# A new order for the first maxima of attention, fewer dummy matmuls among them, and other places for the first loads of W1

## The chip, the cores and the metric

The kernel runs on one core of a Trainium2 chip. The metric is the time of one execution in microseconds on the device; lower is better. Three runs of the kernel before gave 1216.57, 1216.64 and 1218.34 us, median 1216.64. One execution was profiled.

Short names of the engines and queues: PE is TensorE, PEld its weight loads, DVE VectorE, ACT ScalarE, POOL GpSimd, SP SyncE, which here issues most transfers (SPq is its queue).

## The reference

Attention over 8 x 8 heads with pooled queries, then a mixture of eight experts whose tokens are assigned by falling gate score under a cap.

```python
q_pool = q.reshape(B, H, S // 2, 2, D).mean(axis=3)          # B, H, S, D = 8, 8, 1152, 64
scores = q_pool @ k.T / sqrt(D)
scores = scores - max(scores, axis=-1)
attn = exp(scores); attn = attn / (sum(attn) + 1e-09)
x = (attn @ v) as [4608, 512]
logits = x @ w_gate                                          # 8 experts, 576 tokens each at most
for token, expert in order of falling logits: assign if both are free
out[tokens of e] = relu(x[tokens of e] @ w1[e]) @ w2[e]
```

## The kernel before

Attention treats two heads at a time, 32 pairs in all; then the experts run one after the other. Of a pair the work is: loads of keys (KD), queries (QD for the first pair, QS for the others) and values (VD); bounds, sums of absolute values or squares on ACT that give scales (`bounds`); a split of each number into two float16 parts (KH, KL, QH, QL; `split`, `values`); copies of these by SP's transfers into the forms that the score matmuls read (KA, KB, QA, QB, BD; `spread`); the maxima of the scores, one matmul into a PSUM bank and one reduction on DVE for each piece (`max_chunk`), folded by `max_end`, transposed on PE and written into a row of QB by `aug`, where they serve as bounds; then 18 steps (`step`), each with the scores of 128 keys on PE (L793), the exponential on ACT (L796), the low part PM on POOL or DVE (L800) and the weighted sum of values on PE (L810).

The first pair is treated in another way than the rest: its maxima are made head by head, 15 pieces of 384 columns for each head (5 blocks of queries, 3 thirds of the keys; `max_chunk` at n = 0), with a contraction over 64 rows. For the first head the banks rotate over ma, av0, sc0, av1 and sc1, by the number of the piece; for the second head over ma and mb. The written bound needs the constant ndiag, made on DVE by `fill` (L510) from a counter that POOL writes (L508). The later pairs need BD, a block-diagonal copy of QH, for their maxima (L710, L713).

Dummy matmuls of 512 columns (L948) stand in PE's order at the start: ten with the tag "wu" on av1, and as many as AT["wx"] says, 13, with the tag "wx" on av0. Their results are overwritten.

W1 is read once during attention, in 32 loads of 512 KB into the one buffer WB, each with a square on ACT that sums it (`weights`, L472 and L474, one for each pair). A load has to wait until the square of the load before has read WB.

The order of all this work on each engine is set by the class `Cycle`: an operation is given a number from the tables TAU0 (first pair), TAU1, TAU2 and TAU, by its tag and its count, and of the operations whose inputs are written in the order so far the one with the lowest number comes next. The engines and SP's queue each work through their part of that order in turn; an instruction that waits holds all behind it on its engine. In the tables "mm0" and "mr0" are the matmuls and reductions of the first head, "fill" the constants, "ldw" and "wsq" the load and the square of W1, "wx" the dummies, "scv" the scale of the values.

Of the kernel before, what the change touches and what calls it, by code (L numbers as in the profile page):

```python
# [159 lines left out]
class Cycle(Order):  # L160
# [11 lines left out]
    def plan(self):  # L172
# [58 lines left out]
        -31.28967, -16.54009, 11.37296, -165.2382, 7.395536, -8.984111, -4.211814], "expb": [-29.09149,  # L231
        -22.94875, -1.956318, -58.58073, -17.31112, 8.70511, -44.15053, -10.60943, -83.61574], "fill":
# [15 lines left out]
        [-32.42996, -52.99154], "sc": [-118.7466], "scv": [13.52603], "spr": [-12.95725, -60.11802, -17.91313,
        -33.7785, -32.93921, -13.53914, 7.216188, -42.886, 4.220658, -38.88641, -146.5483, -24.13281], "vd":
        [-49.85137, -34.44854], "vh": [8.519713, -90.95726], "vl": [-18.40057, -17.39675], "vs": [-142.1097,  # L250
        -10.46893, -117.9683, -53.38023], "vsh": [-33.54066], "wsq": [12.26831], "wu": [-17.875, -17.555,
        -17.235, -16.915, -16.595, -16.275, -15.955, -15.635, -15.315, -14.995], "wx": [-4.689, -4.369, -3.886,
        -3.403, -3.083, -2.763, -2.28, -1.797, -1.314, -0.994, -0.674, -0.354, -0.034], "x": [26.86098,
        -21.42417]}
TAU1 = {"abs": [-12.63603, -9.007276, -10.61048], "aug": [-9.325879], "augd": [-24.68238, -15.56411], "augt":
# [5 lines left out]
        "expa": [-31.62902, -34.53196, 7.506785, -5.098975, -3.698539, -9.956472, 18.47283, -146.9597,  # L261
        -8.541267], "expb": [-92.73379, -23.81719, -29.00838, -7.55417, 15.52308, 17.65719, 20.07963, -36.40239,
        -8.822007], "fold": [-67.48551], "kd": [-17.85042, -20.86023, -101.4387], "kh": [-21.38899, -13.56883],
        "kl": [-24.3647, -69.39262], "ld": [-38.975, -38.325], "ldq": [-40.925], "ldv": [-39.625], "ldw":
# [8 lines left out]
        7.957536, -30.97699, 26.53293], "qkb": [-134.6881, -19.11279, 4.672508, 7.631733, -18.85315, -7.293164,  # L273
        -146.6946, -45.59129, 22.34192], "ql": [-46.37856], "rc": [-86.19829, -10.06201], "sc": [-61.60109],
        "scv": [-12.29273], "spr": [-7.110299, -82.23665, -9.971891, -10.88851, -4.162817, -38.01306, -24.27872,
        -157.8473, -11.66528, -19.92012, 9.739897, -18.36458], "vd": [-13.48229, -158.5643], "vh": [-13.8261,
        -115.4854], "vl": [-32.5142, -145.3052], "vs": [-102.0759, -147.1307], "vsh": [-42.73812], "wsq":
# [1500 lines left out]
```

## Time and profile before

| | |
|---|---|
| median of three runs | 1216.64 us |
| the profiled execution | 1218.28 us |
| its span, first to last instruction | 1216.5 us |
| PE busy | 1183.1 us, 97% |
| DVE busy | 1000.1 us, 82% |
| ACT busy | 968.8 us, 80% |
| POOL busy | 903.2 us, 74% |

The profile gives the busy time of each engine and, in other views, each instruction with its start. Busy times of PE are modelled at their ends, since matmuls overlap: two matmuls in a row overlap in the rows by some 0.2 us. What stands in brackets behind a row of the order of time is the idle time of the engine before it and what ended that.

### The profile page before, as it was taken

How to read it: one execution, taken by the hardware profiler on the slowest of the kernel's cores; microseconds unless marked ns; L12 is line 12 of the kernel's file. 1: busy time of each engine (PE TensorE's matmuls, PEld its weight loads, DVE VectorE, ACT ScalarE, POOL GpSimd, SP SyncE). 2: the span in 40 equal slices, each digit the busy share in tenths (PEclk: the TensorE clock that was granted, in tenths of full speed). 3: DMA queues.
4: the chain of work that ended last, by engine and by line, in shares of the span. 5: the costliest groups of instructions: out<-in, count | busy, mean ns of one | idle time of the engine just before them, and what ended most of it. 6: DMA issues, size and time to landing. Idle time of an engine off the chain costs nothing.

```text
span 1216.5 us, 39132 instructions
## 1 busy us (share of the span) xinstructions
PE 1183.1 (97%) x15608; PEld 859.7 (71%) x15608; DVE 1000.1 (82%) x2689; ACT 968.8 (80%) x1712; POOL 903.2 (74%) x881
## 2 busy tenths in 40 slices
PE   7889999999999999999999999999999999999998
PEld 2667787787777787877777877776657566575673
DVE  6889999999999999999999996688888898883420
ACT  7868999999999999989988987246887677785851
POOL 6978898898889889888888888244685484676631
PEclk9999999999999999999999999999999999999999
DMA  8666777767777767667668642041453463546301
GB/s 254 155 148 175 174 180 189 175 174 192 174 177 192 168 176 199 166 174 202 163 167 204 162 106 70 22 178 53 165 198 129 147 206 129 165 138 239 118 31 39
DMA packets 131219, 190.84 MB, mean 157 GB/s; under 512 B 50268, under 2 KB 86108, under 8 KB 128732
## 3 DMA queue, kind: packets, MB, share of 16 engines
q1 hardware_dynamic: 117948, 126.75, 39.6%
q0 software_dynamic: 12944, 61.58, 17.3%
q8 instruction: 122, 2.00, 0.7%
q14 instruction: 61, 0.50, 0.1%
q10 hardware_dynamic: 144, 0.02, 0.0%
HBM read 116.41 MB, written 18.87 MB: 111 GB/s over the span
## 4 chain that ended last, share of the span: by engine, by line
PE 82%; DVE 11%; DMA 2%; issue 2%; ACT 1%; SPq 0%; POOL 0%; POOLq 0%; ACTq 0%; DVEq 0%
PE sc L793 21%; PE av L810 19%; PE ph L1661 12%; PE po L1693 11%; PE mb L710 5%; PE ma L710 5%; DVE MX L713 2%; DMA BD<-QH 1%; PE av L857 1%; PE po L1699 1%; PE av L871 1%; PE rt L1264 1%; PE rt L1224 1%; ACT P L796 1%; PE po L1706 1%
## 5 line engine op out<-in xcount | busy, mean ns | idle before, releaser
L800 POOL TENSOR_TENSOR PM<-P 128x576 f16<-128x576 f32 x508 | 611.7, 1265 | 99.1 <-ACT P L796 52.6
L796 ACT ACTIVATE P<-sc,EX 128x576 f32<-128x576 f32 x576 | 412.5, 739 | 77.7 <-PE sc L793 58.1
L810 PEld LDWEIGHTS <-P 128*128 128x128 bf16 x5760 | 293.0, 98 | 30.0 <-issue 1.9
L810 PE MATMUL av<-V,P 128*128 128x65 f16 (+1 forms) x5760 | 301.1, 192 | 0.0
L810 PE MATMUL av<-V,PM 128*128 128x65 f16 x2880 | 292.8, 194 | 0.0
L810 PEld LDWEIGHTS <-PM 128*128 128x128 f16 x2880 | 263.8, 97 | 0.0
L793 PE MATMUL sc<-QB,KB 65*128 65x288 f16 (+1 forms) x1152 | 235.7, 285 | 0.9 <-DMA QB<-AU 0.9
L793 PE MATMUL sc<-QA,KA 128*128 128x288 f16 x1152 | 234.5, 285 | 1.4 <-ACT P L796 1.3
L713 DVE TENSOR_REDUCE MX<-mb 128x1 f32<-128x512 f32 x279 | 190.7, 683 | 27.6 <-PE mb L710 22.6
L713 DVE TENSOR_REDUCE MX<-ma 128x1 f32<-128x512 f32 x279 | 190.6, 683 | 10.7 <-PE ma L710 7.9
L793 PEld LDWEIGHTS <-KA 128*128 128x128 f16 x1152 | 106.1, 97 | 74.2 <-issue 23.6
L1693 PE MATMUL po<-W2H,HX 128*128 128x512 f16 x512 | 155.7, 379 | 0.0
L1661 PE MATMUL ph<-XH,W1H 128*128 128x320 f16 (+1 forms) x512 | 145.5, 286 | 1.2 <-DVE XL L1518 0.9
L1661 PE MATMUL ph<-XH,W1L 128*128 128x320 f16 (+1 forms) x512 | 145.6, 286 | 0.0
L1661 PE MATMUL ph<-XL,W1H 128*128 128x320 f16 (+1 forms) x512 | 145.6, 286 | 0.0
L793 PEld LDWEIGHTS <-KB 65*128 65x128 f16 (+1 forms) x1152 | 112.5, 98 | 30.4 <-issue 1.1
L1693 PEld LDWEIGHTS <-HX 128*128 128x128 f16 x768 | 71.4, 98 | 79.2 <-issue 0.6
L1661 PEld LDWEIGHTS <-W1H 128*128 128x128 f16 x1024 | 97.5, 98 | 28.7 <-issue 5.3
L1715 POOL DMA_INDIRECT out_dram<-OT,idx x40 | 38.9, 971 | 104.8 <-ACT OT L1695 84.4
L710 PE MATMUL ma<-KH,BD 128*128 128x512 f16 x279 | 105.7, 379 | 4.7 <-DMA BD<-QH 2.0
L710 PE MATMUL mb<-KH,BD 128*128 128x512 f16 x279 | 105.5, 378 | 3.2 <-DVE MX L713 1.4
L1613 POOL TENSOR_TENSOR W2L<-W,W2H 128x512 f16<-128x512 f32 x64 | 73.0, 1159 | 35.2 <-ACT W L1611 31.9
(341 smaller groups left out, 2129.9 us busy)
## 6 DMA issues: line engine op xcount, KB each, us to landing
KD<-in_kt_dram SPq DMA_DIRECT2D x64, 288.0 KB
VD<-in_v_dram SPq DMA_DIRECT2D x32, 576.0 KB
WB<-in_w_dram SPq DMA_DIRECT2D x32, 512.0 KB
QA<-QH SPq DMA_DIRECT2D x128, 72.0 KB
KB<-KH SPq DMA_DIRECT2D x64, 144.0 KB
KA<-KH SPq DMA_DIRECT2D x64, 144.0 KB
KA<-KL SPq DMA_DIRECT2D x64, 144.0 KB
x_dram<-X SPq DMA_DIRECT2D x16, 576.0 KB
```

The source lines that it names most:

```text
L710: od.add(t, "PE", 214, lambda: nc.tensor.matmul(m, BD[i][:, j, :], KH[i][:, 512 * c:512 * c + 512], start=True, stop=True), r=bd + [("KH", ...
L713: od.add(t, "DVE", 597, lambda: nc.vector.tensor_reduce(MX[i][:, j, c:c + 1], m, axis=AX.X, op=OP.max), r=[mk], w=[("MX", i, j, c)], tag=" ...
L793: nc.tensor.matmul(c[:, t, :288], a[i][:rows, s, ks], b[i][:rows, s, 288 * t:288 * t + 288], start=first, stop=not first)
L796: od.add(g + 0.1, "ACT", 624, lambda: nc.scalar.activation(p.rearrange("p (t q) -> p t q", t=2), c[:, :, :288], AF.Exp, scale=EX[n % 3][:, ...
L800: od.add(g + 0.2, en, dur, lock=1, fn=lambda: eng.tensor_tensor(pm, p, hi, op=OP.subtract), r=[("P32", g % NP)], w=[("PM", g % NM)], tag="pm")
L810: nc.tensor.matmul(out, w[:, qs], v, start=kb == 0 and j == 0 and y == 0, stop=kb == NKB - 1 and y == 2, skip_group_check=True)
L857: nc.tensor.transpose(m[:, 128 * z:128 * z + 128], X[u][:, 3 * q + z], ident)
L871: nc.tensor.matmul(av[1][32 * q:32 * q + E, :384], wgs[:, c], XT[q].rearrange("p c t -> p (c t)"), start=True, stop=True)
L1613: od.add(tt, "POOL", 1230, lambda o=lo[p], a=raw[p], h=hi[p]: nc.gpsimd.tensor_tensor(o, a, h, op=OP.subtract), r=[key, hk, sk], w=[(nm + ...
L1661: nc.tensor.matmul(p, a[:, d, fs], b[:, d, qs], start=z == 0, stop=z == 11)
L1693: nc.tensor.matmul(o, a[:, z, q0:q0 + 128], b[:, z], start=z == 0 and y == 0, stop=z == 7 and y == 2)
L1715: st = nc.gpsimd.indirect_dma_start(out=out, out_offset=bass.IndirectOffsetOnAxis(ap=idx[i][:n, c:c + 1], axis=0), in_=OT[ob][:n], in_offs ...
```

## The change

Four things, nearly all of them by numbers in the tables:

- The 15 matmuls of the first head get numbers of their own, and the reductions numbers that let each come as soon as its matmul is in the order. The five pieces of the first third of the keys come first, over the five banks in turn, then three of the second third, then the two small matmuls of the values' bound, then the rest.
- AT["wx"] goes from 13 to 5. One of the five stands ahead of the last matmul of the head, four behind it.
- ndiag comes before the first reduction (it now also waits for the limit that `bounds` writes last, EL), and POOL's counter for it comes before the split's work.
- The loads of W1 for the first three pairs, and the square of the first, go elsewhere ("ldw" in three tables, "wsq" in TAU0). The values' scale of the first pair ("scv") has a new number too; on ACT the scale, the first pair's values and the second pair's bounds move up over the square that is gone there.

The diff, cut to its core (the tables are wrapped anew, most of its lines are that):

```diff
-        27.86655, 5.699136, -84.03057], "fold": [-87.75963, -168.3226], "kd": [-5.692977, -1.827225, -13.79063],
-        "kh": [-23.36129, -5.94297], "kl": [-2.127716, -36.39443], "ld": [-17.875, -16.575, -17.225], "ldv":
-        [-15.275], "ldw": [-12.675], "mm0": [-16.51403, -17.39233, -25.94788, -28.2417, -24.44536, -159.4969,
...
+        -16.575, -17.225], "ldv": [-15.275], "ldw": [12.2], "mm0": [-20, -19.95, -4.406, -19.99, -19.94,
+        -4.407, -19.98, -19.93, -4.41, -19.97, -4.412, -4.409, -19.96, -4.411, -4.408], "mm1": [-157.2919,
...
-      15, 16, 17], "d1": 2.0, "cw1": 0.7, "wx": 13, "wy": 0}
+      15, 16, 17], "d1": 2.0, "cw1": 0.7, "wx": 5, "wy": 0}
...
-            od.add(t + .4, "DVE", 370, lambda: nc.vector.tensor_scalar(ndiag, iq, 0.0, -1.0 / UP, op0=OP.is_equal, op1=OP.mult),
-                   r=["iq"], w=["ndiag"], tag="fill")
+            od.add(-55, "DVE", 370, lambda: nc.vector.tensor_scalar(ndiag, iq, 0.0, -1.0 / UP, op0=OP.is_equal, op1=OP.mult),
+                   r=["iq", ("EL", 0)], w=["ndiag"], tag="fill")
```

Lines of the changed kernel lie one lower than those of the kernel before from `routing_tables` on (L704 is L705 there). What the change makes of the order, at three places:

DVE, from the limit of the first pair on; MX is where the reductions write, av_169 is av1, av_168 av0, sc_166 and sc_167 are sc0 and sc1. Before:

```order
L595 TENSOR_SCALAR CB<-EX_116 128x1
L704 TENSOR_REDUCE MX_137<-av_169 128x1
L704 TENSOR_REDUCE MX_137<-sc_166 128x1
L704 TENSOR_REDUCE MX_137<-sc_167 64x1
L704 TENSOR_REDUCE MX_137<-av_168 128x1
L704 TENSOR_REDUCE MX_137<-ma 128x1
L704 TENSOR_REDUCE MX_137<-av_168 128x1
L704 TENSOR_REDUCE MX_137<-av_169 128x1
```

The same place in the changed kernel:

```order
L596 TENSOR_SCALAR CB<-EX_116 128x1
L511 TENSOR_SCALAR ndiag<-scratch 128x640
L705 TENSOR_REDUCE MX_137<-ma 128x1
L705 TENSOR_REDUCE MX_137<-av_168 128x1
L705 TENSOR_REDUCE MX_137<-sc_166 128x1
L705 TENSOR_REDUCE MX_137<-av_169 128x1
L705 TENSOR_REDUCE MX_137<-sc_167 64x1
L705 TENSOR_REDUCE MX_137<-ma 128x1
L571 TENSOR_SCALAR VE_135<-mb 128x1
L576 TENSOR_SCALAR VE_135<-VE_135 128x1
L705 TENSOR_REDUCE MX_137<-av_168 128x1
```

ndiag stands ahead of the reductions, and these go over the five banks in turn.

PE, the last matmuls of the first head; QH and KH are the operands, "ones" and "wide" those of the dummies. Before (behind the last row four more dummies and the transposition follow):

```order
L948 MATMUL av_168<-wide,ones 128x512
L701 LDWEIGHTS QH_89
L701 MATMUL ma<-KH_85,QH_89 128x384
L701 LDWEIGHTS QH_89
L701 MATMUL sc_166<-KH_85,QH_89 128x384
L948 LDWEIGHTS ones
L948 MATMUL av_168<-wide,ones 128x512
```

The same place in the changed kernel (behind the last row three more dummies and the transposition follow):

```order
L702 MATMUL sc_167<-KH_85,QH_89 64x384
L702 LDWEIGHTS QH_89
L702 MATMUL av_168<-KH_85,QH_89 128x384
L949 LDWEIGHTS ones
L949 MATMUL av_168<-wide,ones 128x512
L702 LDWEIGHTS QH_89
L702 MATMUL ma<-KH_85,QH_89 128x384
L949 LDWEIGHTS ones
L949 MATMUL av_168<-wide,ones 128x512
```

One dummy on av0 stands between the last two matmuls, where five stood ahead of both.

SP, the transfers around the fourth pair's BD (BD_102; QS_124 are queries of the fifth pair, the others copies for the third). Before:

```order
L659 DMA QA_98<-QH_90 64x576
L527 DMA QS_124<-in_qt_dram 128x576
L659 DMA QB_99<-QL_91 64x576
L472 DMA WB<-in_w_dram 128x1024
L659 DMA KB_95<-KH_85 64x1152
L659 DMA QB_99<-QL_91 64x576
L638 DMA BD_102<-QH_90 64x9x64 x2
```

The same place in the changed kernel:

```order
L660 DMA QA_98<-QH_90 64x576
L473 DMA WB<-in_w_dram 128x1024
L528 DMA QS_124<-in_qt_dram 128x576
L660 DMA QB_99<-QL_91 64x576
L660 DMA KB_95<-KH_85 64x1152
L660 DMA QB_99<-QL_91 64x576
L639 DMA BD_102<-QH_90 64x9x64 x2
```

Before, the load in this piece is the third of W1; in the changed kernel it is the second, and the third stands later, ahead of KB_96.

## Rows read from the trace of the kernel before

**Rows 1.** The page: busy us, share of the span, instructions of each engine.

```profile
PE 1183.1 (97%) x15608; PEld 859.7 (71%) x15608; DVE 1000.1 (82%) x2689; ACT 968.8 (80%) x1712; POOL 903.2 (74%) x881
```

**Rows 2.** Stretches: length, busy of PE, PEld, DVE, ACT, POOL, PEclk, DMA share, GB/s.

```profile
10.30:13.90 3.60, 3.56 (x10) 0.99 (x10) 2.50 (x5) 3.60 (x7) 3.31 (x4) 1.00 0.98 316
16.20:19.60 3.40, 3.40 (x11) 0.81 (x9) 2.40 (x7) 2.74 (x5) 2.67 (x8) 1.00 1.05 236
...
23.00:32.40 9.40, 8.68 (x53) 4.10 (x52) 7.16 (x17) 7.85 (x14) 7.68 (x7) 1.00 0.53 156
62.00:64.40 2.40, 1.34 (x8) 0.58 (x6) 1.93 (x4) 1.01 (x2) 1.94 (x2) 1.00 0.00 0
...
67.60:68.60 1.00, 1.00 (x25) 0.85 (x22) 0.83 (x5) 0.97 (x4) 0.38 (x1) 1.00 0.08 14
...
72.00:76.00 4.00, 4.00 (x96) 3.47 (x93) 3.95 (x8) 2.79 (x5) 3.55 (x4) 1.00 1.15 205
...
120.00:820.00 700.00, 693.24 (x11512) 552.08 (x11510) 629.32 (x1336) 602.27 (x1039) 583.73 (x524) 1.00 0.65 164
```

**Rows 3.** PE in order of time: start, length, operation, count, [idle before].

```profile
8.09 2.30 PE L948 MATMUL av<-wide,ones 128*128 128x512 bf16 x5
10.32 0.50 PE L701 MATMUL av<-KH,QH 64*128 64x384 f16 x1
...
17.61 2.12 PE L948 MATMUL av<-wide,ones 128*128 128x512 bf16 x5
...
20.09 1.25 PE L948 MATMUL av<-wide,ones 128*128 128x512 bf16 x5
21.61 0.30 PE L755 MATMUL mb<-ident,CM 128*69 128x128 f32 x1 [0.28 <-DVE CM L742]
...
23.20 0.42 PE L793 MATMUL sc<-QA,KA 128*128 128x288 f16 x2
```

**Rows 4.** DVE in order of time, first head's reductions and ndiag.

```profile
10.85 0.56 DVE L704 TENSOR_REDUCE MX<-av 128x1 f32<-128x384 f32 x1 [1.32 <-PE av L701]
...
16.43 0.14 DVE L570 TENSOR_SCALAR VE<-mb 128x1 int32<-128x1 int32 x1
...
17.71 0.55 DVE L704 TENSOR_REDUCE MX<-sc 64x1 f32<-64x384 f32 x1 [0.95 <-PE sc L701]
...
19.11 0.48 DVE L510 TENSOR_SCALAR ndiag<-scratch 128x640 f32<-128x640 int32 x1
20.19 0.56 DVE L704 TENSOR_REDUCE MX<-sc 128x1 f32<-128x384 f32 x1 [0.60 <-PE sc L701]
20.66 0.55 DVE L704 TENSOR_REDUCE MX<-ma 128x1 f32<-128x384 f32 x1
```

**Rows 5.** ACT in order of time, 61 to 70 us.

```profile
61.64 1.37 ACT L796 ACTIVATE P<-sc,EX 128x576 f32<-128x576 f32 x2 [1.67 <-POOL PM L800]
64.44 0.74 ACT L796 ACTIVATE P<-sc,EX 128x576 f32<-128x576 f32 x1 [1.43 <-PE sc L793]
...
66.36 1.06 ACT L474 ACTIVATE VJ<-WB 128x1024 bf16<-128x1024 f32 x1
...
69.27 0.76 ACT L625 ACTIVATE QH<-QS,SC 128x576 f16<-128x576 f32 x1
```

**Rows 6.** SP's queue in order of time: issues of transfers.

```profile
67.59 0.34 SPq L527 DMA_DIRECT2D QS<-in_qt_dram  x1
...
68.62 0.53 SPq L472 DMA_DIRECT2D WB<-in_w_dram  x1
...
70.41 1.38 SPq L638 DMA_DIRECT2D BD<-QH  x2
...
84.78 0.59 SPq L659 DMA_DIRECT2D KB<-KH  x1
```

**Rows 7.** The wait for BD: PE in order of time, then the chain.

```profile
78.93 0.38 PE L710 MATMUL ma<-KH,BD 128*128 128x512 f16 x1 [1.68 <-DMA BD<-QH]
...
71.07 7.73 DMA BD<-QH
```

More of the change, by code (lines that the diff above doesn't have):

```diff
@@ L226 @@
         [-124.0397, -148.4135], "av0a": [11.70915, -1.304429, -29.50539, 21.40864, 9.122039, 19.93749,
[4 rows of a table removed]
-        -31.28967, -16.54009, 11.37296, -165.2382, 7.395536, -8.984111, -4.211814], "expb": [-29.09149,
-        -22.94875, -1.956318, -58.58073, -17.31112, 8.70511, -44.15053, -10.60943, -83.61574], "fill":
[13 rows of a table removed]
-        -0.7874408, -89.24226, -30.95353, -90.94815, 19.75168], "qkb": [-38.71843, -25.8134, -10.06655, 9.20107,
-        -67.31496, -58.03232, -88.79007, 19.41297, 27.0304], "ql": [-118.7245], "qs": [-143.2866], "rc":
@@ L248 @@
[L248 to L252, printed above, removed]
@@ L253 @@
-        -3.403, -3.083, -2.763, -2.28, -1.797, -1.314, -0.994, -0.674, -0.354, -0.034], "x": [26.86098,
-        -21.42417]}
-TAU1 = {"abs": [-12.63603, -9.007276, -10.61048], "aug": [-9.325879], "augd": [-24.68238, -15.56411], "augt":
[5 rows of a table removed]
[L261 to L264, printed above, removed]
[8 rows of a table removed]
[L273 to L277, printed above, removed]
-        [11.82567], "x": [13.33649, -21.05682]}
[5 rows of a table added]
@@ new lines @@
+        "expb": [-29.09149, -22.94875, -1.956318, -58.58073, -17.31112, 8.70511, -44.15053, -10.60943,
+        -83.61574], "fill": [-101.4709, -108.6709, -122.5445, -31.35041, -28.09493, -30, -119, 1.012261,
+        -94.58812, 27.86655, 5.699136, -84.03057], "fold": [-87.75963, -168.3226], "kd": [-5.692977,
+        -1.827225, -13.79063], "kh": [-23.36129, -5.94297], "kl": [-2.127716, -36.39443], "ld": [-17.875,
+        -16.575, -17.225], "ldv": [-15.275], "ldw": [12.2], "mm0": [-20, -19.95, -4.406, -19.99, -19.94,
[8 rows of a table added]
@@ new lines @@
+        -33.38241, -13.43728, -8.625754, -0.787441, -89.24226, -30.95353, -90.94815, 19.75168], "qkb":
[4 rows of a table added]
+        [-18.40057, -17.39675], "vs": [-142.1097, -10.46893, -117.9683, -53.38023], "vsh": [-33.54066], "wsq":
+        [33], "wu": [-17.875, -17.555, -17.235, -16.915, -16.595, -16.275, -15.955, -15.635, -15.315,
+        -14.995], "wx": [-4.689, -4.369, -3.886, -3.403, -3.083, -2.763, -2.28, -1.797, -1.314, -0.994,
+        -0.674, -0.354, -0.034], "x": [26.86098, -21.42417]}
+TAU1 = {"abs": [-12.63603, -9.007276, -10.61048], "aug": [-9.325879], "augd": [-24.68238, -15.56411], "augt":
[6 rows of a table added]
+        -146.9597, -8.541267], "expb": [-92.73379, -23.81719, -29.00838, -7.55417, 15.52308, 17.65719,
[6 rows of a table added]
+        -17.17329, -28.31773, -186.4031, -92.20261, -88.02035, -139.6368, -4.943824, -77.30257], "mre":
[3 rows of a table added]
+        -2.967549, 5.094675, -84.92769, 8.738667, 10.78074, 7.957536, -30.97699, 26.53293], "qkb": [-134.6881,
[6 rows of a table added]
@@ L279 @@
 TAU2 = {"abs": [-28.66554, -33.20308, -33.07647], "aug": [-155.8978], "augd": [-31.13019, -15.26595], "augt":
         [-14.59994], "av0a": [5.912519, -33.47845, -26.79091, -27.48911, -29.13166, -8.697946, -24.82091,
[4 rows of a table removed]
-        [-36.73381, -17.79995, 11.0648, 12.05918, 4.224331, -49.88403, -79.15411, -73.20015, -78.03694], "expb":
-        [5.303638, -28.09439, -86.66189, 11.14589, 13.52404, 0.9933214, -108.1325, 17.65723, -12.04455], "fold":
-        [-76.7964], "kh": [-25.48746, -30.72508], "kl": [-85.91257, -137.1086], "ld": [-43.77507, -60.36052],
@@ L288 @@
-        "ldq": [-155.8887], "ldv": [-44.13215], "ldw": [-36.80441], "me": [-14.41274, -10.50764, -4.941736],
[7 rows of a table removed]
-        [3.525368, 5.485969, 7.082238, -29.81771, 16.89603, 17.62602, 19.72256, 21.49451, 25.15933], "qkb":
[4 rows of a table removed]
-        -140.0679], "vsh": [-156.7671], "wsq": [25.35071], "x": [-88.3642, 9.707762]}
[4 rows of a table added]
+        [-34.60962], "expa": [-36.73381, -17.79995, 11.0648, 12.05918, 4.224331, -49.88403, -79.15411,
+        -73.20015, -78.03694], "expb": [5.303638, -28.09439, -86.66189, 11.14589, 13.52404, 0.993321,
@@ new lines @@
+        -108.1325, 17.65723, -12.04455], "fold": [-76.7964], "kh": [-25.48746, -30.72508], "kl": [-85.91257,
+        -137.1086], "ld": [-43.77507, -60.36052], "ldq": [-155.8887], "ldv": [-44.13215], "ldw": [2.8], "me":
[8 rows of a table added]
+        19.72256, 21.49451, 25.15933], "qkb": [4.228648, -8.449217, 6.503895, 8.362543, 2.06596, 19.41358,
+        21.0541, 27.28868, 28.96957], "ql": [-13.86136], "rc": [-14.19222, -72.26224], "sc": [-157.8417],
+        "scv": [-26.20257], "spr": [-19.00547, -5.537296, -11.12926, -16.76412, -6.043836, -10.26983,
@@ L302 @@
+        -53.42223, -16.37789, -0.047992, -17.85246, -27.80794, -15.06558], "vh": [-108.6609, -34.0504], "vl":
+        [2.133735, -132.8829], "vs": [-32.43098, -140.0679], "vsh": [-156.7671], "wsq": [25.35071], "x":
+        [-88.3642, 9.707762]}
 AT = {"load": -11.1, "vload": -12.4, "split": -11.0, "bound": -10.3, "bq": 0.1, "bv": -0.1, "bs": 0.1, "spread": 4.1,
```

91 rows, old and new, of tables (TAU0, TAU1, TAU2) are left out of this document.

## The prediction

> **What bounds the kernel now.** I read the page's shares first: TensorE (PE) is busy 97% of the span, VectorE (DVE) 82% [rows 1]. Then the table of stretches: from 120 to 820 us PE is busy 693.24 of 700.00 us, but in 62 to 64.4 us only 1.34 of 2.40 [rows 2]. PE works in program order and is full later, so a microsecond is won or lost only where it still waits, in the first 100 us; what its queue gains there reaches the end. Everything the change moves lies there. So I read that stretch engine by engine, in order of time: PE [rows 3], DVE [rows 4], ScalarE (ACT) [rows 5], the SP queue [rows 6], and at last the one wait on a transfer that PE shows [rows 7].
>
> Two places count. **Place one** is the first head's maxima: 15 reductions on DVE from 10.85 us to the last start at 20.66 [rows 4], then PE's transposition at 21.61, then the first scores at 23.20 [rows 3]. **Place two** is PE's wait of 1.68 us for BD of the fourth pair, ended at 78.93; that transfer took 7.73 us [rows 7].
>
> **The clock at place one.** The granted clock reads 1.00 in every stretch, but the rows of one shape do not agree: five matmuls of 512 columns are 2.30 us long at 8.09, 2.12 at 17.61, and 1.25 at 20.09 [rows 3]. That is about 0.43 us each, 512 columns at 1.2 GHz, and then 0.21, at 2.4. So the clock rose shortly before 20 us. Before it PE was busy 3.40 of 3.40 us, with seven dummies in it, while 3.56 of 3.60 us of mostly 64-row maxima at 10.3 did not raise it [rows 2].
>
> **Part 1, the order over five banks.** Before, the maxima wait for matmuls that stand behind dummies and in shared banks: DVE is idle 1.32 us before the first, 0.95 before the one at 17.71, 0.60 before the one at 20.19, and the constant ndiag (0.48) stands among them at 19.11 [rows 4]. The first start stays at 10.85, since the five dummies ahead of it stay. A reduction takes the engine 0.47 us (20.19 to 20.66). After, fourteen reductions follow without a hole, as each matmul's bank was read three or more places earlier, and the two small steps of the values' bound cost some 0.15 each (0.14 at 16.43 [rows 4]): the fourteenth starts at 10.85 + 13 x 0.47 + 0.31 = 17.27 and ends 0.55 later, at 17.82. The fifteenth is not free: one dummy on the same bank stands between the fourteenth's matmul and its own on PE, so it waits for reduction 14, the dummy, its matmul and two hand-overs of some 0.05. At 2.4 GHz (0.21 + 0.18) it starts at about 18.35, at 1.2 GHz (0.43 + 0.32) at 18.7. Against 20.66 that is 2.3 or 2.0 us.
>
> **Part 2, the dummies.** Eight of thirteen go, four remain between the last maximum and the transposition. At 2.4 GHz they take 0.86 us and end before DVE has folded the maxima (0.95 after the last start, 21.61 against 20.66), so the transposition gains the whole 2.3. At 1.2 GHz they take 1.72 behind a matmul that ends at about 18.6: transposition at 20.35, a gain of 1.25. ndiag early costs nothing: it falls into the 1.32 us of idle DVE, and its counter is moved into POOL time before 10 us.
>
> **How the profiled execution stands to the median.** It took 1218.28 us; three runs gave 1216.57, 1216.64 and 1218.34. The difference, 1.64, is what eight dummies lose by the lower clock: 8 x 0.21 = 1.7. So I take it that in the median run the clock rose before 15.7 us, and the transposition came near 20.0 there. Then the new order is worth less to the median run than to the profiled one: 2.3 - 1.64, about 0.7 us. The clock then has to survive a stretch (14 to 18 us) in which PE only makes a matmul of 0.18 us for each reduction of 0.47. The nearest row is 62 to 64.4 us, busy 1.34 of 2.40, after which the matmuls still run at 2.4 GHz; it is denser, and this is the forecast's weak point.
>
> [...]
>
> **Part 3, W1's loads.** Each is 128 x 1024 numbers of 4 bytes, 512 KB [rows 5]. The first leaves the opening burst and comes after the values of the third pair; its square leaves ACT's opening and goes between the exponentials of 61.64 and 64.44, where ACT is idle 1.43 us before 64.44 and the square takes 1.06 [rows 5]: hidden. If that hole closes, it costs up to the 1.06. The second load is issued when that square ends, about 64.1, where nothing moves (0 GB/s in 62 to 64.4 [rows 2]); SP stood still there until QS at 67.59 [rows 6], so nothing is held up. Its own square stands on ACT at 66.36 [rows 5]. A load moves some 1.0 us after its issue (QS of 67.59: 14 GB/s in 67.6 to 68.6 us), and 512 KB take 1.7 us at the 316 GB/s of 10.3 to 13.9 us and 2.6 at the 205 of 72 to 76 [rows 2]: it lands between 66.8 and 67.7, ACT waits 0.4 to 1.3 us (I take 0.8), and QH at 69.27 and BD's issue at 70.41 come that much later. The third load leaves its place at 68.62, ahead of BD, and goes in front of the keys issued at 84.78 [rows 6]: 512 KB less before BD, 2.6 us at 205 GB/s. BD lands 2.6 - 0.8 = 1.8 earlier, which clears PE's 1.68; I take 1.4, because the delayed exponentials push PE's scores before it by some 0.3. At its new place the load delays keys of the fourth pair, which are hidden behind that pair's maxima, since those only begin at 78.93 [rows 7]; if that cover fails, it costs up to 2.6.
>
> **Sum.** Against the profiled execution with the clock up early: 2.3 + 1.4 = 3.7, 1218.28 - 3.7 = 1214.6. Against the median run: 0.7 + 1.4 = 2.1, 1216.64 - 2.1 = 1214.5. I forecast **1214.6**, 0.17% less, just inside the 0.2% (2.4 us) that a measurement of this kernel can tell from no change. Its own range is 1213.8 to 1215.6.
>
> **Rivals.**
> 1. The clock rises late. With eight dummies gone, PE's first dense work is the scores beside the second head's maxima. From 23 to 32.4 us PE does 13 matmuls of 384 and 36 of 288 columns, 15,360 columns: 6.4 us at 2.4 GHz, 12.8 at 1.2, in 9.40 us of which it was busy 8.68 [rows 2]. If the first third or so runs at 1.2, it costs 1.5 to 2, some of it in waits that are there anyway; I take 1.3. Against the profiled execution: -1.25 + 1.3 - 1.4, 1216.9. For it: in the profiled execution the rise came right behind seven dummies of 128 rows. Against it: 8 to 14 us is as dense as before, and the run of scores behind the transposition is dense too.
> 2. The second load of W1 lands late (W1 packets at 205 GB/s and below), ACT is held two microseconds or more, and BD gains nothing: 1216.64 - 0.7 = 1215.9, or 1216.5 with part of the hold on the path.
> 3. Slower: the clock stays at 1.2 GHz through that stretch and two microseconds of the dense values' matmuls behind it. Then PE is the bound of all of it, 12.8 us instead of 9.4, 3.4 lost, and 1.0 in the two behind, less 1.25 and 1.4: 1218.28 + 1.75 = 1220.0. It makes the kernel slower than the median before if the rise comes after about 28 us (2.0 lost: 1217.6).
> 4. The two groups of runs are not the clock's doing, and place one gains its 2.3 in the median run too: 1216.64 - 2.3 - 1.4 = 1212.9.
> 5. The order does not do what it says (a hole before reduction 9, or 11, from PE's small bound matmuls ahead of them): 0.3 to 0.5 of place one is lost, 1215.0; it lies in the forecast's own range.
>
> **How the numbers follow.** Chances: forecast (with 5) 0.48, rival 1 0.18, rival 2 0.12, rival 3 0.10, rival 4 0.12. The range goes from rival 4 to above rivals 1 and 2: 1212.8 to 1217.3, leaving out rival 3 and a little. Faster by over 0.2% (under 1214.2): rival 4 and half of the forecast's own, 0.36. Slower (over 1219.1): rival 3 and its neighbourhood, 0.10. The rest, 0.54, is within 0.2%.
>
> **What would show it.** In the profile after: fourteen reductions in a row from 10.85 to about 17.8, the fifteenth after a gap of some 0.5; the transposition at 19.2 to 20.4; the dummies' length there (0.21 or 0.43 each) and that of the score matmuls behind, which part rival 1 and 3 from the forecast; the square at about 66.4 less the shift, with ACT's wait for WB before it; BD landed before PE asks. Wrong would be a first reduction later than 10.85, PE still waiting over 1 us for BD, or score matmuls at 1.2 GHz after 23 us.

## The result: slower, and where the time went

The changed kernel took 1225.09 us (median of seven runs, 1220.16 to 1229.46), the kernel before 1217.32 beside it (median of seven): a ratio of 1.0056, with a 95% interval of 1.0040 to 1.0072 (the quotient of the two medians is 1.0064; the ratio with its interval is what is given below too). That is slower by 0.4 to 0.7%, where 1214.6 was forecast. The profiled execution of the changed kernel took 1229.46 us and is the slowest of its seven, 4.4 us above their median; what is read from it below is more than the median run lost.

The page, busy times as in [rows 1]:

```profile
PE 1190.8 (97%) x15600; PEld 863.4 (70%) x15600; DVE 1003.8 (82%) x2689; ACT 969.1 (79%) x1712; POOL 903.9 (74%) x881
```

PE has eight matmuls less and is busy 7.7 us longer. The best first step with two traces is to find the same matmul in both, counted from the end of the program, and to note how much later it starts. This table does it (us later than in the profile of before; the heads are times in that profile). The other kernels are the experiments below.

| kernel | 28.0 | 37.6 | 66.9 | 72.2 | 80.9 | 95.1 | 108.1 | 120.9 |
|---|---|---|---|---|---|---|---|---|
| changed kernel | 3.1 | 7.0 | 7.0 | 8.8 | 7.0 | 6.1 | 10.9 | 10.8 |
| few_dummies | 3.7 | 7.1 | 7.1 | 7.1 | 5.7 | 5.7 | 5.7 | 5.7 |
| w1_back | 3.0 | 6.8 | 6.8 | 6.8 | 5.0 | 4.2 | 4.3 | 4.4 |
| dense_end | 1.9 | 1.9 | 1.9 | 1.9 | 3.8 | 3.8 | 3.8 | 3.9 |
| warm_start | 2.3 | 6.1 | 6.1 | 6.1 | 4.5 | 4.5 | 4.5 | 4.5 |
| free_bank | 4.3 | 5.7 | 5.7 | 9.0 | 7.1 | 6.2 | 7.3 | 7.4 |
| hold | -0.5 | 0.9 | 0.9 | 0.9 | -0.8 | -1.7 | -1.6 | -1.6 |
| hold_third | -1.6 | -1.6 | -1.6 | -1.6 | -3.3 | -4.2 | -4.0 | -3.4 |
| hold_small | -1.0 | 0.4 | 0.8 | 0.8 | -0.9 | -1.8 | -1.1 | -1.0 |
| w1_only | 0.7 | 3.6 | 3.6 | 7.0 | 5.1 | 4.2 | 7.7 | 8.3 |
| third_only | -0.8 | -0.8 | -0.8 | -0.8 | -2.6 | -3.5 | -2.8 | -2.7 |
| first_two | 0.7 | 3.5 | 3.5 | 7.0 | 5.2 | 4.3 | 4.4 | 4.4 |
| light_third | 0.4 | 0.4 | 0.6 | 4.2 | 2.3 | 1.4 | 1.5 | 1.5 |

From -0.3 to 0.8 us of each row comes from the opening and not from the place read: the opening loads land at other times, and the first maximum starts between 10.1 and 11.1 us (10.32 in [rows 3], 11.08 in the changed kernel). In the changed kernel the time goes at three places: 23 to 42 us, about 70, and about 108. Seven microseconds are gone by 37.6.

PE of the changed kernel, in order of time:

```profile
18.50 0.59 PE L949 MATMUL av<-wide,ones 128*128 128x512 bf16 x1 [0.95 <-DVE MX L705]
...
19.45 1.89 PE L949 MATMUL av<-wide,ones 128*128 128x512 bf16 x4
21.13 0.42 PE L756 MATMUL mb<-ident,CM 128*69 128x128 f32 x1
...
22.99 0.66 PE L794 MATMUL sc<-QA,KA 128*128 128x288 f16 x2
...
37.03 0.69 PE L794 MATMUL sc<-QB,KB 69*128 69x288 f16 x2
...
42.78 0.41 PE L794 MATMUL sc<-QA,KA 128*128 128x288 f16 x2
```

Pairs of score matmuls took 0.42 us in [rows 3]; here they take 0.66 to 0.69 from 22.99 to 37.03 and only at 42.78 the 0.41 of the higher clock. The dummies at 19.45 take 0.43 each. So the clock stayed low through the whole stretch. (w1_only, an experiment below, has pairs of the same 0.66 to 0.69 in 31 to 34 us, and there the column of the clock reads 0.50. The prediction's 1.2 and 2.4 GHz are the columns a ns worked out from the rows, 512 in 0.43 and in 0.21 us.) How much that held back is seen in the stretches (columns as in [rows 2]):

```profile
23.00:32.40 9.40, 9.40 (x38) 4.15 (x37) 4.42 (x12) 4.94 (x9) 5.69 (x5) 1.00 0.45 137
32.40:41.00 8.60, 8.27 (x71) 4.45 (x70) 3.80 (x9) 6.28 (x9) 7.14 (x7) 1.00 0.39 84
```

In 23 to 32.4 us PE did 38 matmuls and was busy all the time, where it did 53 in 8.68 us before [rows 2]; DVE fell from 7.16 us busy to 4.42. PE had become the bound. The column of the clock says 1.00 all the same, here as in 10.30 to 13.90 us of before, behind five dummies of 2.30 us ([rows 2] and [rows 3]): in these traces it does not show the low stretch with which an execution begins, the length of a known shape does.

The maxima themselves did what was forecast. DVE in order of time:

```profile
11.61 0.56 DVE L705 TENSOR_REDUCE MX<-ma 128x1 f32<-128x384 f32 x1 [0.92 <-PE ma L702]
...
17.91 0.54 DVE L705 TENSOR_REDUCE MX<-av 128x1 f32<-128x384 f32 x1
19.55 0.56 DVE L705 TENSOR_REDUCE MX<-ma 128x1 f32<-128x384 f32 x1 [1.11 <-PE ma L702]
```

Fourteen reductions follow each other without a hole, the fifteenth starts 7.94 us after the first (7.85 was worked out for the low clock, and it was 9.81 before [rows 4]).

At the second place, W1's loads: ACT, SP's queue, and PE, each in order of time.

```profile
69.91 1.05 ACT L475 ACTIVATE VJ<-WB 128x1024 bf16<-128x1024 f32 x1
...
75.12 1.06 ACT L475 ACTIVATE VJ<-WB 128x1024 bf16<-128x1024 f32 x1 [1.79 <-DMA WB<-in_w_dram]
```

```profile
71.08 0.33 SPq L473 DMA_DIRECT2D WB<-in_w_dram  x1
...
78.82 1.30 SPq L639 DMA_DIRECT2D BD<-QH  x2
```

```profile
76.95 0.41 PE L794 MATMUL sc<-QA,KA 128*128 128x288 f16 x2 [1.72 <-ACT P L797]
...
85.86 0.38 PE L711 MATMUL ma<-KH,BD 128*128 128x512 f16 x1
```

The second load was issued at 71.08 and landed 3.96 us later by the chain of waits; ACT stood 1.79 us for it, and PE 1.72 us behind ACT. PE's wait of 1.68 for BD [rows 7] is gone in this execution: the matmul that ended it at 78.93 is, counted from the end, the one at 85.86, with no idle time before it. Whether the moved load is the reason is taken up under w1_back.

At the third place DVE, POOL and PE, and two stretches:

```profile
104.89 1.74 DVE L653 SCALAR_TENSOR_TENSOR KL<-KD,SC,KH 128x576 f16<-128x576 f32 x1
...
107.57 4.71 DVE L653 SCALAR_TENSOR_TENSOR KL<-KD,SC,KH 128x576 f16<-128x576 f32 x1
```

```profile
104.88 1.15 POOL L801 TENSOR_TENSOR PM<-P 128x576 f16<-128x576 f32 x1 [0.68 <-ACT P L797]
107.34 0.92 POOL L529 DMA_DIRECT2D QS<-in_qt_dram  x1 [1.32 <-DMA QS<-in_qt_dram]
108.01 3.65 POOL L801 TENSOR_TENSOR PM<-P 128x576 f16<-128x576 f32 x3
```

```profile
112.59 0.38 PE L711 MATMUL mb<-KH,BD 128*128 128x512 f16 x1 [3.03 <-DVE AU L767]
```

```profile
108.00:112.00 4.00, 1.55 (x11) 0.53 (x11) 4.00 (x1) 1.60 (x3) 3.65 (x4) 1.00 0.69 147
112.00:116.00 4.00, 3.41 (x34) 2.44 (x34) 2.61 (x6) 2.48 (x5) 1.15 (x1) 0.69 0.34 74
```

POOL waited 1.32 us for a late transfer, had three products queued behind it, and ran from 107.34 to 111.66 without a pause. DVE's KL, 0.81 us long where nothing disturbs it (the median of 60 in before), began at 107.57 and took 4.71. PE waited 3.03 us for what follows KL, and the granted clock fell (0.69 in 112 to 116). KL ended 0.6 us behind the last of POOL's row (112.28 and 111.66), and the 1.74 of 104.89 ended 0.6 us behind its one product (106.63 and 106.03); what ties the two engines together was not shown. It is a single case: of the 60 KL on DVE in each of the fourteen profiles no other is longer than 1.8 us. 1.74 or 1.75 beside one product is in every profile, and in that of before the next KL ended at 102.91, 0.6 us behind the first of two products in a row (101.15 to 102.29) and inside the row of the second (102.26 to 103.91):

```profile
98.61 1.74 DVE L652 SCALAR_TENSOR_TENSOR KL<-KD,SC,KH 128x576 f16<-128x576 f32 x1
...
101.28 1.63 DVE L652 SCALAR_TENSOR_TENSOR KL<-KD,SC,KH 128x576 f16<-128x576 f32 x1
```

### The profile page after: what moved, and what is told of

Same layout as the page of the kernel before. It is cut to its first block, busy times and chain, and to the rows that moved or that the text cites. A ratio compares the mean times of both kernels' runs of the same rounds, so it can differ in the third digit from the quotient of the medians.

```text
span 1227.7 us, 39114 instructions
## 1 busy us (share of the span) xinstructions
PE 1190.8 (97%) x15600; PEld 863.4 (70%) x15600; DVE 1003.8 (82%) x2689; ACT 969.1 (79%) x1712; POOL 903.9 (74%) x881
## 4 chain that ended last, share of the span: by engine, by line
PE 81%; DVE 11%; issue 2%; DMA 2%; ACT 2%; POOL 1%; SPq 0%; POOLq 0%; ACTq 0%; DVEq 0%
PE sc L794 21%; PE av L811 19%; PE ph L1662 12%; PE po L1694 11%; PE mb L711 5%; PE ma L711 5%; DVE MX L714 2%; PE av L858 1%; PE po L1700 1%; ACT P L797 1%; PE av L872 1%; PE rt L1265 1%; DMA BD<-QH 1%; PE rt L1225 1%; PE po L1707 1%
## 5 line engine op out<-in xcount | busy, mean ns | idle before, releaser
L794 PE MATMUL sc<-QA,KA 128*128 128x288 f16 x1152 | 237.1, 287 | 3.1 <-ACT P L797 3.0
L794 PE MATMUL sc<-QB,KB 65*128 65x288 f16 (+1 forms) x1152 | 238.5, 288 | 0.0
```

Source lines behind the costliest of these rows:

```text
L794: nc.tensor.matmul(c[:, t, :288], a[i][:rows, s, ks], b[i][:rows, s, 288 * t:288 * t + 288], start=first, stop=not first)
```

## The experiments

Each is timed beside the kernel before on the same chip, and the ratios are compared. On some of these chips the kernel before took 1243.81 to 1249.07 us (medians), on the others 1217.32 and 1218.19, and nearly all of that lies behind the table (third_only is 2.7 us early at 120.9, its span 26.5 us longer than that of before), so times from different chips are not.

**Theory A**: eight dummies fewer leave PE without the dense work that brings the clock up, and it runs at the low clock to 41 us. **Theory B**: the new order does it, whatever the dummies. **Theory C**: W1's moved loads make the later transfers late; **theory D**: only ACT's wait for the second load costs. Each kernel was profiled once, so a difference between two profiles can be the chance of one execution.

### few_dummies, w1_back and w1_only: one part each

```diff
-      15, 16, 17], "d1": 2.0, "cw1": 0.7, "wx": 13, "wy": 0}
+      15, 16, 17], "d1": 2.0, "cw1": 0.7, "wx": 5, "wy": 0}
```

> The kernel before with one edit: five of the thirteen dummies on av0 instead of thirteen; order of the maxima, ndiag and W1's loads stay. Theory A (the missing dummies leave PE at 1.2 GHz until about 40 us): score matmuls behind 23 us read 0.66 us a pair instead of 0.42, PE is 5 to 7 us late by 60 us, the median is 1221 to 1225. Theory B (the new order or W1's loads cost the time, the dummies don't): the maxima end earlier by up to the dummies' time, pairs at 0.42, 1215 to 1217.5.

Ratio 1.0052 (1.0031 to 1.0073). PE in order of time:

```profile
21.70 0.45 PE L755 MATMUL mb<-ident,CM 128*69 128x128 f32 x1 [1.46 <-DVE CM L742]
...
23.60 0.66 PE L793 MATMUL sc<-QA,KA 128*128 128x288 f16 x2
...
37.64 0.69 PE L793 MATMUL sc<-QB,KB 69*128 69x288 f16 x2
...
42.88 0.41 PE L793 MATMUL sc<-QA,KA 128*128 128x288 f16 x2
```

The order of before with five dummies loses 7.1 us by 37.6, as the changed kernel does. That is theory A, and theory B falls.

w1_back is the changed kernel with the W1 part undone, w1_only the kernel before with that part alone:

```diff
 TAU0
-"ldw": [12.2] ... "scv": [-1.7] ... "wsq": [33]
+"ldw": [-12.675] ... "scv": [13.52603] ... "wsq": [12.26831]
 TAU1
-"ldw": [11]
+"ldw": [-66.81886]
 TAU2
-"ldw": [2.8]
+"ldw": [-36.80441]
```

> The changed kernel with W1's loads, the first square and the values' scale back at the numbers of before; the new order, five dummies and the early ndiag stay. Theory A (clock): pairs of score matmuls at 0.66 until about 40 us, PE 6 to 7 us late at 60 us, 1222 to 1225. Theory C (W1's loads): 1215 to 1218.

> The kernel before with the W1 part alone: loads of the first three pairs, the first square and the values' scale at their new numbers. Theory A (clock): pairs of score matmuls at 0.42 behind 23 us, ACT waits 0.8 to 1.8 us for the second load, PE's wait of 1.68 for BD goes and is paid by the wait ahead of it: 1216 to 1218. Theory C (the moved loads start a chain of late transfers, with a stretched DVE instruction behind it): 4 us or more lost between 70 and 110 us, 1220 to 1225.

w1_back: 1.0039 (1.0011 to 1.0067), 6.8 us late at 37.6, 4.4 at the end of the table. w1_only: 1.0025 (1.0007 to 1.0043), slower too. The two parts add to 0.64%, and the whole change is 0.56%; the three intervals overlap. The profile of w1_only is the slowest of its twelve runs, 6.8 us above their median, so the 8.3 us at the end of its row are more than the W1 part costs as a rule. ACT of w1_only, and PE:

```profile
71.76 1.06 ACT L473 ACTIVATE VJ<-WB 128x1024 bf16<-128x1024 f32 x1 [1.86 <-DMA WB<-in_w_dram]
```

```profile
108.74 0.39 PE L709 MATMUL ma<-KH,BD 128*128 128x512 f16 x1 [1.91 <-DMA BD<-QH]
```

```profile
27.00:31.00 4.00, 3.32 (x23) 1.70 (x21) 3.14 (x10) 3.70 (x9) 4.00 (x5) 1.00 0.38 74
31.00:34.40 3.40, 3.40 (x12) 1.11 (x11) 1.55 (x3) 2.41 (x4) 3.40 (x3) 0.50 0.32 48
```

The wait on ACT recurs (1.86), and so does a loss behind 95 us (4.2 to 8.3), here with a wait of 1.91 for a later BD, as theory C has it. The 2.9 us that it loses earlier, up to 37.6, are a fall of the clock at 31 us (0.50), of which more below.

w1_back shows one thing more. It regains 1.75 us between 72.2 and 80.9 with the loads where they were: PE does not wait for BD there. That it is late is not the reason, since BD is issued later by as much (77.19, and 70.41 in [rows 6]). SP's queue and PE of w1_back, PE of hold (an experiment below, W1 as before, PE only 0.9 late), the chain of few_dummies and PE of dense_end:

```profile
77.19 1.42 SPq L638 DMA_DIRECT2D BD<-QH  x2
...
83.89 0.38 PE L710 MATMUL ma<-KH,BD 128*128 128x512 f16 x1
...
78.02 0.38 PE L709 MATMUL ma<-KH,BD 128*128 128x512 f16 x1
...
78.18 6.30 DMA BD<-QH
...
81.68 0.58 PE L710 MATMUL ma<-KH,BD 128*128 128x512 f16 x1 [2.52 <-DMA QB<-AU]
```

In all these kernels but w1_only, first_two, light_third and free_bank, where it is 7.8, PE asks for BD 6.0 to 6.4 us after the issue of its second half. What differs is the transfer. By the updates of its semaphore in the traces, with the third load issued 1.8 us ahead of it, that half landed 7.73 us after its issue in before, 8.57 in dense_end, 6.30 in few_dummies, and 5.4 to 6.1 in w1_back, hold and warm_start; PE waited 1.68, 2.52 (put down to another transfer), 0.24, and three times less than 0.1. So the 1.68 of [rows 7] was one draw out of 0 to 2.5. In the other eight BD landed 2.4 to 4.4 us after its issue and PE never waited. What the W1 part could win at BD is therefore 0 to 2.5 us, and in the changed kernel its wait for WB, 1.76 us, stands against that.

### free_bank and dense_end: dummies back, in other places

```diff
+    for _ in range(8):
+        od.add(-45, "PE", 320, lambda: nc.tensor.matmul(sc[0][:, 1, :512], ones, wide[:, :512], start=True, stop=True), w=[("sc", 0, 1)], tag="wz")
```

> The changed kernel plus eight dummies of 512 columns on the second bank of sc0, which nothing reads or writes in these stretches, one behind each of the maxima from the ninth on and three ahead of the last: no reduction has to wait for a bank because of them, but PE is dense from 14 us to the transposition. Theory A (clock): matmuls of 0.21 to 0.22 us for 512 columns before the transposition, pairs of scores at 0.42 behind it, 5 to 7 us of the loss gone: 1217 to 1219. Theory B or C: nothing comes back, 1224 to 1226.

Ratio 1.0103 (1.0071 to 1.0135): worse, against every theory as I had priced it. PE:

```profile
15.57 0.59 PE L951 MATMUL sc<-wide,ones 128*128 128x512 bf16 x1 [1.08 <-DVE MX L705]
...
24.09 1.89 PE L949 MATMUL av<-wide,ones 128*128 128x512 bf16 x4
25.77 0.41 PE L756 MATMUL mb<-ident,CM 128*69 128x128 f32 x1
```

The experiment was not the one I meant. The dummies do wait for the reductions of sc0's first bank (1.08), as the two banks are one tile. PE was not dense, the dummies at 24.09 still took 0.43 each, and the transposition came 4.6 us later than in the changed kernel. Behind it the clock was up (a pair of scores at 27.47 took 0.42; 5.7 us late at 37.6, most of it that delay). The profile is one of the two short runs of six (1256.1 and 1256.3); the others took 1261.7 to 1265.4, and what they lost beyond it was not seen.

dense_end is w1_back with thirteen dummies in the new order, twelve of them in one row:

```diff
-"wx": 5
+"wx": 13
```

> The kernel of w1_back (new order of the maxima, early ndiag, W1's loads as before) with thirteen dummies instead of five: one stands ahead of the last maximum, the other twelve in a row behind it, ahead of the transposition. Theory A (it is the eight dummies, as dense work for PE, that bring the clock up): the twelve begin at 0.43 us each and the clock rises among them or right behind, pairs of score matmuls read 0.42 by 25 us at the latest; the transposition comes 1.7 to 3.4 us later than in w1_back, but behind 42 us PE is 2.5 to 4.5 us late against the kernel before where w1_back was 6.8: adding work makes the kernel 2 to 4 us faster than w1_back. Theory B (the dummies' number does not matter, the new order keeps the clock low): pairs at 0.66 until about 40 us and 10 us late there.

Ratio 1.0003 (0.9990 to 1.0017). PE:

```profile
18.89 4.84 PE L948 MATMUL av<-wide,ones 128*128 128x512 bf16 x12
23.56 0.27 PE L755 MATMUL mb<-ident,CM 128*69 128x128 f32 x1
...
25.12 0.42 PE L793 MATMUL sc<-QA,KA 128*128 128x288 f16 x2
```

Eight useless matmuls more, 3.0 us of delay for the transposition (counted from the first maximum), and the ratio is 0.36% lower than that of w1_back: the pairs behind read 0.42, and PE is 1.9 us late at 37.6 where w1_back was 6.8. That settles theory A by the rows; the two ratios' intervals still touch. Between 72.2 and 80.9 this profile loses another 1.9 us, by the wait of 2.52 for BD shown above, and it is the slowest of its ten runs.

### warm_start, hold, hold_third, hold_small: can the clock be had earlier?

warm_start adds to w1_back four dummies in the opening; hold adds twelve more among the maxima, on mb, with new numbers for three of the maxima; hold_third is hold with the third load of W1 moved, hold_small the same with dummies of 256 columns.

```diff
+    for _ in range(4):
+        od.add(-45, "PE", 320, lambda: nc.tensor.matmul(sc[0][:, 1, :512], ones, wide[:, :512], start=True, stop=True), w=[("sc", 0, 1)], tag="wz")
+    for t, k in ((-59, 6), (-55, 6)):
+        for _ in range(k):
+            od.add(t, "PE", 320, lambda: nc.tensor.matmul(mb[:, :512], ones, wide[:, :512], start=True, stop=True), w=["mb"], tag="wy")
```

> The kernel of w1_back with four more dummies of 512 columns among the first five, in the opening where PE idles from 5.64 to 8 us; the five behind the first bounds and the five at the end of the maxima stay. Theory A1 (dense work anywhere brings the clock up, and it lasts through the maxima): dummies of 0.21 us before 11 us, maxima at 0.33 in the rows, transposition at 19.2 to 19.8, pairs of scores at 0.42: 1 to 3 us faster than the kernel before. Theory A2 (it comes up, but the maxima of 64 rows with gaps behind 14 us let it fall again): 0.21 before 12 us, and 0.43 at the dummies behind 17 us, pairs at 0.66, slow as w1_back.

Ratio 1.0042 (1.0017 to 1.0067). PE in order of time, then stretches:

```profile
8.45 1.24 PE L948 MATMUL av<-wide,ones 128*128 128x512 bf16 x5
...
17.71 0.59 PE L948 MATMUL av<-wide,ones 128*128 128x512 bf16 x1 [0.95 <-DVE MX L704]
```

```profile
13.00:17.00 4.00, 2.87 (x7) 0.75 (x7) 3.85 (x11) 3.94 (x9) 4.00 (x7) 0.51 0.98 233
...
23.00:32.40 9.40, 9.40 (x37) 4.00 (x36) 3.75 (x10) 5.32 (x10) 5.68 (x5) 0.50 0.39 126
...
41.00:45.00 4.00, 3.29 (x21) 2.04 (x22) 3.50 (x7) 2.11 (x3) 1.82 (x3) 1.00 0.64 179
```

Five dummies in 1.24 us at 8.45: the clock was up. In 13 to 17 us it is down again (0.51), and it stays down to 40 us though PE is busy 9.40 of 9.40 us in between. In this execution the new order, with one matmul of 64 rows for each reduction, did not hold the clock.

> The kernel of warm_start with twelve more dummies of 512 columns, on mb, which nobody reads between the first bounds and the values' bound nor between that and the transposition: one between any two maxima of the first head from the third on, so that PE always has work of 128 rows beside the reductions; three maxima get numbers of their own for that. W1's loads as before. Theory A (dense work of 128 rows brings the clock up in the opening, and it is the sparse maxima that let it fall): dummies of 0.21 us from 12 us at the latest to the transposition, which comes at 18.8 to 19.8; pairs of score matmuls at 0.42; PE 1.5 to 2.8 us earlier than before at 28 us, 2 to 6 us faster than warm_start. If the dummies do not hold the clock: maxima 0.75 us apart, transposition at 23 us or later, pairs of 0.66, slower than warm_start.

> The kernel of hold with the third load of W1 behind the fourth pair's BD as in third_only. If both gains add: PE's wait for BD of 1.7 us goes too, 1.3 to 1.8 us less than hold, 3 to 4.5 us (0.25 to 0.35%) less than the kernel before. If the earlier clock makes PE ask for BD earlier than the transfers can bring it, the wait stays at 1 us or more and the two kernels are within 0.7 us.

hold: 1.0012 (0.9987 to 1.0037); hold_third: 1.0018 (0.9988 to 1.0048): neither can be told from the kernel before. PE of hold, then of hold_third:

```profile
12.94 0.39 PE L952 MATMUL mb<-wide,ones 128*128 128x512 bf16 x1
13.27 0.33 PE L700 MATMUL ma<-KH,QH 64*128 64x384 f16 x1
13.53 0.39 PE L952 MATMUL mb<-wide,ones 128*128 128x512 bf16 x1
```

```profile
20.02 0.30 PE L754 MATMUL mb<-ident,CM 128*69 128x128 f32 x1
```

In these executions the clock held through the maxima with the dummies among them (a maximum took 0.33 in the rows, 0.50 in w1_back at 18.90), the transposition came at 20.02 in hold_third, and by 95 us its PE was 4.2 us ahead of the kernel before. In hold the clock fell later, from 32.2 to 35.6 us, and PE lost 1.4 us between 28.0 and 37.6. The medians do not show it: some runs of hold_third took 1230 to 1231 us, most 1216 to 1217, and one profile cannot say what the long ones did. My 0.25 to 0.35% was not met.

> The kernel of hold_third with the twelve dummies among the maxima at 256 columns instead of 512. In hold_third a maximum and its dummy took PE 0.59 us where a reduction takes DVE 0.47, so PE set the pace. If the smaller ones still hold the clock: maxima 0.47 to 0.50 apart, transposition 0.8 to 1.4 us earlier against the first reduction than in hold_third, and 0.5 to 1.4 us less time than it. If they do not: the clock falls among the maxima in the profile, dummies of 0.43 us behind 17 us and pairs of scores at 0.66, 5 us slower than hold_third.

Ratio 1.0045 (1.0028 to 1.0061). The smaller dummies did set the maxima 0.48 us apart (12.16 and 12.64 for two dummies in order of time), but the clock fell among them in the profile, as the second case said: the dummy at 17.59 took 0.59 us in the rows, the four at 18.75 1.89.

### third_only, first_two, light_third: which load

third_only is the kernel before with the third load's number alone (TAU2's "ldw": [2.8]); first_two has the rest of the W1 part and not that.

> The kernel before with one edit: the third load of W1 goes from its place ahead of the fourth pair's BD to a place among the keys of the fourth pair, about 16 us later; nothing else moves on any engine. Theory C (this load, at its new place, makes the transfers of 92 to 105 us late): PE's wait of 1.68 for BD goes, and 2 to 4 us are lost between 92 and 112 us, 1 to 3 us slower than before. Theory D (only the second load and ACT's wait for it cost): 1.0 to 1.7 us faster than before and nothing lost between 92 and 112.

> The kernel before with the first two loads of W1, the first square and the values' scale at their new numbers and the third load where it was. Theory C: ACT waits 0.8 to 1.9 us for the second load, SP's queue waits with the third load until the second square is over, BD comes 3 us or more later than before and PE waits 3 us or more for it, and nothing is lost between 92 and 112 us. Theory D: the same wait on ACT and a loss between 92 and 112 us all the same.

third_only: 0.9997 (0.9979 to 1.0014). PE:

```profile
76.27 0.38 PE L710 MATMUL ma<-KH,BD 128*128 128x512 f16 x1
```

The wait for BD is gone (1.75 us between 72.2 and 80.9 in the table), as the third term of the forecast said, though w1_back and hold show the same gain without the move; and 0.8 us are lost behind 95, 0.67 of them in a wait for the next pair's BD: mostly theory D. The timing cannot tell 1.7 us from nothing on that chip. first_two, timed once: ACT waits 1.96 us for WB, PE is 3.5 us later by 72.2, and nothing is lost behind 95 us. So neither part alone makes a loss of 4 us behind 95 us, and neither theory was right as put. Both together do not always make it either: free_bank has both and loses 1.1 us there.

light_third tests what the third load adds to it. It is w1_only, and that load brings 64 columns of its 1024 (the sum of squares of that piece is then another):

```diff
-od.add(t, "SP", 650, lambda: nc.sync.dma_start(WB, w1[...]), w=["WB"],
+od.add(t, "SP", 650, lambda: nc.sync.dma_start(*((WB[:, :64], w1[..., :64]) if n == 2 else (WB, w1[...]))), w=["WB"],
```

> The kernel of w1_only, but the third load of W1 brings only 64 of its 1024 columns, so 480 KB less move at its new place (the sum of squares of that piece is wrong for it); order, count of instructions and waits stay. Theory C1 (the loss between 92 and 112 us comes of that load's bytes among the transfers of the next pairs): PE loses under 1 us between 95 and 112 us, where w1_only went from 4.2 to 8.3 us late; ACT's wait for the second load of 1.8 us stays. Theory C2 (the bytes do not matter; the transfers are late since the whole queue behind ACT's wait is): 3 to 4 us lost there all the same.

ACT in order of time:

```profile
68.91 1.06 ACT L473 ACTIVATE VJ<-WB 128x1024 bf16<-128x1024 f32 x1 [2.01 <-DMA WB<-in_w_dram]
```

ACT's wait stays (2.01), and between 95.1 and 120.9 PE loses 0.1 us where w1_only lost 4.0. That speaks for the bytes of the third load (C1), though it is one profile against one. The other rows of the table agree: from 95.1 to 120.9 PE loses 0.8 us in third_only, hold_third and hold_small, 1.1 in free_bank, 4.0 in w1_only and 4.7 in the changed kernel, all with that load's bytes at the new place, and at most 0.3 in the seven kernels without them. That the loss is larger behind ACT's wait is likely and not shown, as free_bank has that wait too (1.75). In w1_only and in the changed kernel a part of it is a fall of the clock right behind the wait, 3.4 us long in each (0.69 in 108 to 112 us of w1_only, and in 112 to 116 of the changed kernel). In its profile and in those of w1_only and first_two PE loses 3.4 to 3.6 us just ahead of 72.2, twice ACT's wait; the rest is matmuls at the lower clock right behind it, as in w1_only's 76 to 79 us:

```profile
76.00:79.00 3.00, 3.00 (x46) 2.55 (x45) 2.48 (x4) 2.06 (x4) 1.49 (x2) 0.53 0.50 84
```

## Why the prediction was wrong, step by step

**Part 1, the order: right.** The fifteenth reduction starts 7.94 us behind the first, 7.85 forecast for the lower clock; no hole before reduction 9 or 11, so rival 5 falls. The early ndiag lies in idle time, as forecast: 0.92 us of idle DVE are left between it and the first reduction.

**Part 2, the dummies: right up to the transposition.** From the first reduction to the transposition it is 9.52 us (21.13 less 11.61), 9.50 by the working at the low clock, 10.76 before. The gain of 1.25 is there; the first reduction came 0.76 later, by the opening load and not by the change.

**The median run: the step that failed first.** I took 1218.28 against 1216.57 for the dummies' clock and concluded that the median run had the clock up before 15.7 us. The profiles of the other kernels with the order of before and thirteen dummies (w1_only, third_only, first_two, light_third) do not say so: the five dummies ahead of the last maxima took 2.31, 2.06, 2.32 and 2.31 us in them, as the 2.12 of [rows 3], and the five behind 1.25 to 1.59: the clock rose there in each of them. (In third_only it had been up for a few maxima before, 0.32 to 0.33 us each at 11.92 to 14.69, and was down again.) Three run times in two groups were no ground for a term of 1.6 us, and the seven that now stand (1216.57, 1216.64, 1217.21, 1217.32, 1218.15, 1218.34 and 1222.81) show no two groups.

**"The clock then has to survive": the wrong question.** It had not risen yet (in warm_start, where it had, it did not survive, as was feared: 0.51 in 13 to 17 us). The place in which it rose before was the place from which the change took eight dummies. I gave the rivals in which it rises late 0.28 together; by the profile, with 2.12 us for the five dummies at 17.61 and 1.25 for those at 20.09 [rows 3], the late rise was the likelier case. Rival 3 was the mechanism, and its price was too small: I let the low clock end at 34 us and charged 4.4 us for it. It lasted to 41 us: at the low clock PE reached the values' matmuls only at 38.11 (before at 32.55), and the first pair behind them, at 42.78, is the first at 0.41. It cost 7.5: PE is 7.0 late at 37.6, from a transposition that was 0.5 early. That the clock hangs on the dummies is shown by two pairs of kernels that differ in them alone (pairs of 0.42 behind thirteen of them in before and in dense_end, of 0.66 behind five in few_dummies and in w1_back); what in that work brings it up is not: PE was busy 9.40 of 9.40 us from 23 to 32.4 in the changed kernel, and the clock stayed low.

**Part 3, W1's loads: two terms mis-sized, one term missing.** The first square stood in ACT's idle time, as said. The second load landed 3.96 us after its issue, not 2.7 to 3.6, and ACT waited 1.79 us against the 0.4 to 1.3 of the forecast (1.75 to 2.01 in four other kernels): that was rival 2's ground. The wait for BD was taken from one execution as if it were the kernel's: BD did land earlier, but the 1.68 us to be had were 0 to 2.5 in the six profiles with the load just ahead of BD, and in three of these PE waited less than 0.1 us without any move. Missing was the loss behind: "that cover fails, up to 2.6" was put at the fourth pair's keys, and what failed was the transfers of the pair behind, 4.7 us in the profile of the changed kernel, 4.0 in w1_only and 1.1 in free_bank.

**The sum of the measured parts.** Order and dummies 0.39%, W1 0.25%, together 0.64%; the change 0.56%. By w1_back's 0.39% the start is the larger part, some 4.7 us of 1217; the interval (0.11 to 0.67%) overlaps that of w1_only, and it is the rows, 7.0 us late by 37.6, that make the start the first cause.

What stays open: why the clock sometimes holds between 28 and 31 us and sometimes falls for 3 to 7 us (it held in before, third_only, dense_end, hold_third and light_third, and fell in w1_only, first_two and hold_small, in hold at 32 and in free_bank at 36, with PE no less busy: 2.37 of 3.00 us in before, 3.32 of 4.00 in w1_only); and how many runs of the changed kernel have the 4.71 us of KL, since only the slowest was profiled, and in w1_only, free_bank and the rest no KL is that long.

## What to carry to other kernels

Before taking idle-looking work from PE, find the row at which a known shape halves its time, and try what stands ahead of it: here eight dummies of up to 0.43 us each were taken from there, and the price was not their own time but the stretch behind them to 41 us, with pairs of scores at 0.66 instead of 0.42 and PE 7 us late. A wait that the change is to remove should be looked for in several executions: a transfer that lands late in one profile (BD, 7.73 us) need not in the next (5.4 to 6.1 in three), and then there is nothing to win. And two moved transfers that cost little one by one can meet (behind 95 us 0.8 us in third_only, 0.1 in first_two, 4.0 with both in w1_only); sum their bytes at the place where both are late.

## What the hardware showed beyond that

- KL on DVE, an instruction with three operands, took 0.81 us by itself, about 1.74 beside a single POOL product of 1.15 that started just ahead of it (in every profile), and once 4.71 beside a POOL transfer issue and three products without a pause. It is not always the whole row: in before one ended after 1.63, inside the second of two products in a row (101.28).
- In hold, matmuls of 64 and of 128 rows in turn cost more than the sum: a maximum of 384 columns and a dummy of 512 came every 0.59 us (12.94 to 13.53), at the higher clock, where such a dummy by itself takes 0.21 us [rows 3] and such a maximum 0.16 (10.07, 10.23 and 10.39 are the starts of three in a row in hold_third). Each pair costs some 0.2 us more; rows, number format and weights change together there, and which of them costs it was not tested.
- The clock fell in 13 to 17 us of warm_start (0.51) with PE busy 2.87 of 4.00 us, and stayed low (0.50) with PE busy all of 23 to 32.4.
